# Loading and rounding v by GpSimd, a chunk of four units at a time

## The chip, the core and the metric

The kernel runs on one core of a Trainium2 chip. The core has five engines with a queue of instructions each: TensorE (PE in the profile; its weight loads are PEld), VectorE (DVE), ScalarE (ACT), GpSimd (POOL) and SyncE (SP). Each queue is worked off in order, and engines wait for one another by semaphores. Sixteen DMA engines, common to all queues, move data between device memory and the on-chip memory. The metric is device microseconds of one execution, lower is better; the profile is one execution seen by the hardware profiler.

## What is computed

Two layers follow each other. The first is a linear attention with a decaying state, over batch 4, 8 heads, 768 steps and a head dimension of 48:

```python
for t in range(S):
    cur = np.einsum('bhd,bhe->bhde', u[None] * kt, vt)
    y[:, :, t] = np.einsum('bhd,bhde->bhe', rt, state + cur)
    state = wt[:, :, :, None] * state + np.einsum('bhd,bhe->bhde', kt, vt)
```

The second takes y as 3072 tokens of 384 features and computes h = y w_in (384 to 1024), solu = h softmax(h), a layer norm of solu with gains g_ln, and the product with w_out (1024 to 384). All inputs and the output are float32 in device memory.

## The kernel before

The 768 steps are cut into six chunks of C = 128, and a chunk of one batch is a *unit*: 24 units, unit i being chunk i // 4 of batch i % 4. In a unit the 128 steps lie on the partitions, and the 8 heads times 48 features, 384 columns, along the free axis. Four units in a row are thus one chunk of all batches. The state st of a batch goes from one of its units to the next.

For each unit the kernel loads w, k, r and v (192 KB each, in pieces of 48 float32, 192 bytes). The rows in order of work, with the stage's name in the program: lw takes the logarithm of w (ACT); cum sums it with two matmuls, ex exponentiates (ACT) and kp multiplies into k and r (DVE); krk and krr transpose on PE and kr copies the result (DVE or ACT). M makes the scores, m copies them with the causal mask, on DVE in one step or on ACT with the mask sel behind it on POOL. p, q and qh on POOL and dg on DVE make the bonus term r·u·k of each head and step, and dv (POOL) multiplies it into v. Y is the attention output on PE: it reads the masked scores and v, and for a unit marked `i` also dv by a matmul; otherwise dv is added in the copy y on DVE. S is the new state on PE, with v as its moving operand, and et and st end it. X and xT transpose y, H is the first product of the second layer, e its exponential (ACT), he the product (DVE), hq the square, ea a half sum of e (POOL), Oa and Ob the second product with the sums of the norm, sq, qm, lv and o the norm, and out the store (SP).

v goes through two stages of its own. LV is a load by SP into one of seven float32 buffers v_in, and vb a rounding copy into one of ten bf16 buffers vb. A suffix in the order says which engine makes the copy: 12 on POOL (`vb2.p`), six on DVE (`vb1.d`), six on ACT (`vb0.a`). Readers of vb are S, Y and dv (lines 360, 406 and 434).

Nothing is scheduled by a compiler. One string, ORDER (lines 21 to 67), lists every stage of every unit, and the loop at its end (lines 550 to 553) emits them one by one. The class InOrder (lines 72 to 90) makes each instruction follow the last of its own engine, so each engine's queue has the order of the string. That is why most rows of the profile bear line 86, the line in InOrder that makes the call: a row is told by the tiles that it writes and reads, not by its line. A stage that comes too early in the string makes its engine wait with everything behind it. All loads and stores stand in SP's queue, in the order of the string, and a load waits there until its buffer is free.

Around the start of the string, SP's loads are LW2, LU0, LW1, LW3, LR2, LK2, LV2, LR1, LK1, LW0, LV1, LW4, LG0, LR0, LK0, LR3, LK3, LR4, LV0, LK4, then the weights (LI, LO), then LV3, LW6, LV4 and so on. Unit 2 is the first to be computed, then 1 and 0.

Of the kernel before, what the change touches and what calls it, by code (L numbers as in the profile page):

```python
# [8 lines left out]
F32 = mybir.dt.float32  # L9
BF16 = mybir.dt.bfloat16  # L10
# [10 lines left out]
ORDER = """  # L21
LW2 LU0 ik0 lw2 hot5.4 cum2.0 LW1 lw1 us0.7 ih0 LW3 lw3 cum3.2 LR2 uc0 ex2 LK2 p2 LV2 vb2.p kp2 hot4.4 krk2.6 krr2
LR1 LK1 cum1.4 LW0 ex1 kp1 kr2.d hot1.0 S2.7 lw0 et2 LV1 vb1.d LW4 st2 p1 q1 hot2.0 krk1.1 krr1 q2 qh2 dg2 LG0
kr1.a M2.4 ex3 hot1.0 M1.6 m1.d dv2 LR0 LK0 p0 q0 cum0.0 ex0 lw4 cum4.6 ex4 kp0 krk0.1 krr0 LR3 gs0.0 gc0 dg1
m2.d Y2.i0 kr0.d LK3 p3 LR4 LV0 vb0.a dg0 dv1 kp3 Y1.i5 hot3.1 krk3.4 krr3 LK4 kp4 M0.2 m0.d krk4.1 y1.a X1.5
krr4 y2.a X2.0 dv0 xT2.d hot1.6 Y0.n7 y0.d kr3.a M3.2 hot1.0 X0.6 S1.4 p4 q3 kr4.a xT1.a xT0.a LI2 LI1 wi1.a
M4.0 m4.a et1 LI0 S0.5 et0 wi0.d m3.d LO1 wi2.p H1.6 e1 gw5.a H2.0 e2 H0.2 LO0 gw2.a q4 qh4 dg4 qh3 dg3 gw4.p
gw7.p LV3 vb3.p dv3 sel4 LW6 e0 gw6.d st1 LV4 vb4.p he1 lw6 dv4 gw1.d LW5 gw0.d gw3.d mn0.4 mc0 ce5.p ce6.p
Y3.i7 ce4.p he2 st0 he0 cum6.0 y3.a ce7.p hot1.5 X3.6 lw5 xT3.a ce3.d LK6 LR6 p6 Y4.n5 LR5 LK5 ce2.d hq0.a ex6
LW7 cum5.2 H3.6 p5 y4.d ex5 ce1.d ce0.d Oa0.5 kp6 krk6.1 krr6 S4.0 hq1.d Oa1.4 kp5 krk5.3 krr5 X4.2 Ob1 e3 he3  # L30
LV5 q6 q5 kr5.d hq2.a et4 st4 M5.6 kr6.a M6.0 xT4.d lw7 cum7.2 hq3.a sq1 m6.a m5.d dg5 vb5.d qm1 dv5 Ob0 ex7 sq0
qm0 S3.7 qh6 LR7 LK7 p7 kp7 et3 lv1 st3 lv0 H4.0 Y5.n6 y5.d LR9 LK8 o1.d e4 krk7.3 krr7 Oa2.2 he4 X5.7 q7 kr7.d
LW9 lw9 o0.a LK9 p9 LW8 lw8 S5.6 et5 cum9.4 ex9 Ob2 sq2 LR8 p8 st5 dg6 kp9 qm2 LV6 xT5.a LV9 vb6.p dv6 sel6
cum8.0 ex8 kp8 hq4.a LV7 LV11 out1 LW10 dg7 vb7.p dv7 Oa3.3 vb9.a lv2 H5.6 e5 M7.4 m7.d he5 q8 krk9.1 LK10 krr9
kr9.a S9.0 et9 Ob3 sq3 st9 q9 qm3 o2.a out0 ea5.p Y6.i5 y6.a LV8 LR10 Y7.n4 y7.d LW11 LW12 krk8.1 M9.6 lw10 lv3
X6.2 xT6.a m9.d o3.a krr8 LV10 out3 out2 kr8.d qh9 dg9 dg8 hq5.d cum10.4 ex10 kp10 S6.0 vb11.d et6 X7.2 xT7.a
st6 p10 vb8.d dv8 dv9 H6.6 e6 he6 H7.2 lw11 e7 he7 M8.4 m8.a Oa5.1 Y9.n0 Ob5 sq5 y9.d cum11.6 ex11 krk10.5 krr10
qm5 kr10.d S7.4 et7 st7 Oa4.3 hq6.d lv5 lw12 o5.a X9.2 sel8 Y8.i0 vb10.p y8.a LK11 LR11 kp11 xT9.d q10 dg10 p11
M10.4 m10.a sel10 S10.1 et10 st10 dv10 S8.0 et8 S11.7 et11 X8.6 xT8.a LK12 LW13 cum12.4 q11 ex12 lw13 st11 st8
Ob4 sq4 qm4 LW14 LR12 kp12 p12 lw14 lv4 o4.a out5 LK13 LV12 LR13 Y10.n2 dg11 y10.d H8.6 e8 krk12.1 krk11.0 krr11  # L40
krr12 kr12.d he8 kr11.a q12 qh12 cum13.4 H9.2 vb12.p S12.1 ex13 p13 q13 ea7.p dg12 kp13 dv11 LW16 LR14 LK14 e9
he9 et12 st12 M12.6 m12.a Oa6.0 X10.5 xT10.a krk13.4 krr13 kr13.a M11.6 m11.d ea8.p dv12 sel12 p14 cum14.2 ex14
q14 out4 Ob6 sq6 hq8.d M13.4 m13.d LV13 hq7.a LW15 lw15 lw16 kp14 vb13.d H10.6 dg13 qm6 LW18 lw18 Y11.n1 y11.d
Oa8.5 LK16 LR15 LR16 LK15 e10 he10 hq9.a krk14.4 Y12.i3 krr14 lv6 qh14 kr14.d p15 ea10.p dv13 LR18 LV14 vb14.p
q15 qh15 LK18 p18 Ob8 sq8 qm8 y12.a S13.2 et13 st13 o6.a lv8 X11.1 xT11.d cum16.6 ex16 X12.3 hq10.d LW19 kp16
Oa9.4 cum15.0 xT12.a Ob9 ex15 kp15 sq9 o8.a dg14 dv14 qm9 M14.2 m14.a sel14 krk16.7 Oa7.6 krr16 kr16.d lv9 o9.d
cum18.0 ex18 kp18 Ob7 LV15 S14.5 et14 st14 krk15.3 krr15 kr15.d LK19 Y13.i2 lw19 cum19.0 krk18.7 p16 q16 vb15.a
S15.4 y13.a sq7 qm7 dg15 X13.5 xT13.d ex19 LR19 kp19 lv7 o7.a q18 krr18 kr18.d H11.2 et15 st15 krk19.5 krr19
kr19.d LW17 lw17 cum17.0 e11 he11 ex17 ea11.p out8 LK17 LR17 p17 kp17 H12.6 e12 he12 hq11.a p19 H13.4 e13 Oa10.3
Y14.n2 M16.0 m16.a dg16 q19 dv15 y14.d ea12.p ea13.p M15.6 m15.d he13 Ob10 sq10 X14.2 out9 Oa11.1 LW20 qm10 lw20  # L50
cum20.6 hq12.d krk17.0 krr17 out6 out7 LV16 vb16.a dv16 xT14.a S16.2 LR20 ex20 LK20 dg18 et16 st16 lv10 o10.a
H14.4 e14 kp20 Ob11 sq11 kr17.d LK23 qm11 lv11 o11.a Oa12.2 krk20.3 krr20 kr20.a he14 sel16 Y16.n7 y16.d Y15.n6
y15.d M19.4 m19.a M18.0 m18.d Ob12 X15.7 xT15.a q17 hq13.d LV19 LW21 LV17 X16.3 xT16.a ea14.p vb19.a M17.4 m17.d
sq12 LK22 out10 qm12 dg17 qh19 vb17.p sel19 p20 hq14.a LW22 LV20 q20 qh20 dv17 M20.0 LV21 m20.d out11 LK21 H15.6
e15 he15 lw22 ea15.p H16.4 LV18 vb18.p dv18 LR21 p21 lw21 Oa14.3 Y17.n1 LR22 LV23 q21 dg19 dv19 Ob14 LR23 p23
p22 e16 he16 lv12 Oa13.0 LW23 o12.a out12 sq14 qm14 hq15.d vb20.a lv14 dg20 dv20 y17.d cum21.6 ex21 Ob13 cum22.4
sq13 ex22 LV22 vb22.p ea16.p o14.d out14 Y18.n2 y18.d Oa15.1 X18.3 qm13 kp22 lv13 xT18.d X17.2 xT17.a kp21 Ob15
sq15 qm15 S18.5 et18 st18 Y19.n4 y19.d lv15 o15.a out15 o13.a krk22.2 S17.3 et17 lw23 H18.6 e18 ea18.p hq16.d
vb21.d st17 Y20.n5 y20.d X19.4 xT19.d krr22 kr22.a H17.0 he18 hq18.d cum23.4 ex23 kp23 Oa16.3 e17 ea17.p he17
krk21.2 krr21 kr21.a H19.6 e19 krk23.5 X20.4 krr23 q22 qh21 vb23.p out13 xT20.a kr23.a he19 Oa18.2 Ob16 sq16  # L60
M21.0 q23 ea19.p qh23 dg22 dv22 m21.a sel21 qm16 lv16 M22.6 hq19.a M23.4 Ob18 sq18 dg21 H20.0 o16.a out16 m22.d
m23.d Oa19.7 Y22.n6 qm18 lv18 hq17.d Ob19 S19.5 dg23 dv23 e20 Oa17.4 y22.d X22.3 he20 et19 st19 xT22.d dv21
Y21.n6 Ob17 y21.d sq19 o18.a sq17 qm17 lv17 Y23.n1 out18 qm19 lv19 X21.0 xT21.d H22.2 o17.a e22 out17 ea20.p
y23.d H21.0 X23.5 xT23.a e21 hq20.d o19.d out19 Oa20.6 he22 hq22.d H23.4 e23 he21 hq21.d Ob20 sq20 qm20 lv20
o20.a out20 ea22.p Oa22.7 ea21.p Oa21.3 he23 hq23.d Ob22 sq22 qm22 lv22 Ob21 sq21 qm21 lv21 o21.d o22.a out22
out21 ea23.p Oa23.2 Ob23 sq23 qm23 lv23 o23.a out23
"""

NIO, NLW, NKP, NWK = 7, 10, 6, 4
# [24 lines left out]
def kernel(  # L94
# [26 lines left out]

    nc.scalar.preload_act_table_set("natural_log_exp_and_others")
# [27 lines left out]
    v_t = ring("v_in", NIO, [C, H, 64], F32)  # L150
# [4 lines left out]
    g_rows = consts.tile([KF, 128], F32)  # L155

# [41 lines left out]
    vb_t = ring("vb", NLW, [C, H, D], BF16)  # L198
# [15 lines left out]
    qm_t = ring("qm", NWK, [C, 1], F32)  # L214
    lv_t = ring("lv", NWK, [C, 1], F32)
# [30 lines left out]
    def load_w(i, x):  # L246
        sp.dma_start(out=w_t[i % NIO][:, :, :D], in_=rows_of(w, i))

    def load_k(i, x):
        sp.dma_start(out=kr_t[i % NIO][:, 0, :, :D], in_=rows_of(k, i))  # L250

    def load_r(i, x):
        sp.dma_start(out=kr_t[i % NIO][:, 1, :, :D], in_=rows_of(r, i))

    def load_v(i, x):
        sp.dma_start(out=v_t[i % NIO][:, :, :D], in_=rows_of(v, i))

    def load_u(i, x):
        sp.dma_start(out=u_row, in_=u.rearrange("(o h) d -> o (h d)", o=1))

    def load_g(i, x):
        sp.dma_start(out=g_rows, in_=moe_g_ln.rearrange("(ko ki) -> ko ki", ki=128))

    def load_w_in(j, x):
        sp.dma_start(out=win_f[:, j, :], in_=moe_w_in[j * 128:(j + 1) * 128, :])

    def load_w_out(j, x):
        part = slice(j * KF // 2, (j + 1) * KF // 2)
        sp.dma_start(out=wout_f[:, part, :],
                     in_=moe_w_out.rearrange("(ko ki) d -> ki ko d", ki=128)[:, part, :])  # L270
# [79 lines left out]
    def v_cast(i, x):  # L350
        copy = {"a": act.copy, "d": dve.tensor_copy, "p": pool.tensor_copy}[x]
        copy(out=vb_t[i % NLW], in_=v_t[i % NIO][:, :, :D])

# [4 lines left out]
    def bonus_v(i, x):  # L358
        dg = dg_t[i % NWK]
        pool.tensor_mul(out=dv_t[i % NKP], in0=vb_t[i % NLW], in1=dg.unsqueeze(2).to_broadcast([C, H, D]))  # L360
# [16 lines left out]
    def transposed_copy(i, x):  # L377
        copy = {"a": act.copy, "d": dve.tensor_copy}[x]
        copy(out=kr_s[i % NKP], in_=live[i]["kr_ps"])

# [22 lines left out]
    def attend(i, x):  # L403
        L = live[i]
        c, b = units[i]
        m, kr, vb = m_t[i % NWK], kr_s[i % NKP], vb_t[i % NLW]
        y_ps = L["y_ps"] = bank([C, DM], F32, x[-1], "y_ps")
        first = True
        if x[0] == "i":
# [67 lines left out]
    def hidden_exp(i, x):  # L477
        act.activation(out=e_t[i % NWK], in_=live[i]["h_ps"], func=EXP)
# [105 lines left out]
```

## Time and profile before

| what | value |
|---|---|
| median of 2 runs | 155.07 us (154.83 to 155.32) |
| span of the profiled execution | 152.4 us |
| what lies around the span, by the median of the runs | 155.07 - 152.4 = 2.7 us |
| granted TensorE clock, mean over the span | 0.975 |
| DMA queue of SP | 104,802 packets, 26.75 MB, 77.4% of 16 engines' span |
| of these, packets of v | 24 loads of 128 x 8 pieces = 24,576 |
| copies vb on POOL, 12 | 6.3 us, mean 522 ns |
| copies vb on DVE, 6 | 3.8 us, mean 635 ns |
| copies vb on ACT, 6 | 3.1 us, mean 510 ns |
| v loads, issue to landing | 3.6 us median, 3.1 to 6.7 |

The profile gives no time of the profiled execution but its span, from the first instruction to the last; the runs' times are longer by what lies around it. In the profile "idle before" is the time that an engine stood still ahead of an instruction, with what ended that wait. The chain that ended last is followed back from the last instruction, at each step to what released it. DMA shares can go above 1 in a stretch, because records of packets overlap.

### The profile page before, as it was taken

Reading aid. Unit: us, or ns where it says so; the run is one execution under the profiler, and the core shown is the slowest. Engines: PE = TensorE matmul, PEld = TensorE weight load, DVE = VectorE, ACT = ScalarE, POOL = GpSimd, SP = SyncE. Lnnn points to the kernel's source line nnn. Section 1 sums busy time; section 2 is a strip of 40 time slices with the busy share of each in tenths; the row PEclk is TensorE's granted clock in tenths of the full one; section 3 lists DMA queues with packets and bytes.
Section 4 is the critical chain, followed back from the end, with each engine's and each line's share of the span. In section 5 each row is a group of like instructions: output and inputs, shape, how many; then the busy total and the mean of one; then the engine's idle time right before and its main releaser. Section 6 shows DMA issues by size and latency. Waiting matters only on the chain.

```text
span 152.4 us, 5172 instructions
## 1 busy us (share of the span) xinstructions
PE 136.4 (90%) x2093; PEld 105.5 (69%) x2093; DVE 131.8 (87%) x227; ACT 120.0 (79%) x247; POOL 119.0 (78%) x149
## 2 busy tenths in 40 slices
PE   6777598968999999999998999999799999999970
PEld 1242365936778889779776689887686988889740
DVE  5029968899999999998999999999999999988940
ACT  4526648869888999799998889998988789938661
POOL 7268986799909994899999997799889979973600
PEclk9959969999999999999999999999999999999998
DMA  3999999989979999989897989995998110112023
GB/s 76 218 216 211 217 334 377 254 175 223 216 151 216 220 204 229 206 177 224 194 203 144 228 195 275 199 199 136 241 205 210 63 45 4 44 63 103 4 79 127
DMA packets 104825, 27.06 MB, mean 178 GB/s; under 512 B 100314, under 2 KB 104419, under 8 KB 104803
## 3 DMA queue, kind: packets, MB, share of 16 engines
q1 hardware_dynamic: 104802, 26.75, 77.4%
q8 instruction: 16, 0.26, 0.7%
q14 instruction: 7, 0.05, 0.1%
HBM read 22.03 MB, written 4.72 MB: 176 GB/s over the span
## 4 chain that ended last, share of the span: by engine, by line
PE 53%; DVE 23%; SPq 8%; ACT 6%; issue 3%; DMA 2%; POOL 1%; DVEq 0%; POOLq 0%
PE ps L86 53%; SPq L86 7%; DVE he L86 6%; DVE m L86 4%; DVE kp L86 4%; DVE w L86 3%; DMA kr_in<-in_k_dram 2%; DVE kr L86 1%; DVE hq L86 1%; DVE y L86 1%; DVE st L86 1%; ACT ps L86 1%; ACT o L86 1%; DVE dg L86 1%; ACT win_sb L86 1%
## 5 line engine op out<-in xcount | busy, mean ns | idle before, releaser
L86 PE MATMUL ps<-w,he 128*128 128x385 bf16 x192 | 44.5, 325 | 1.0 <-DVE w L86 0.7
L86 PE MATMUL ps<-xT,win_sb 128*128 128x128 bf16 x576 | 35.5, 219 | 1.1 <-DVE qm L86 0.8
L86 PEld LDWEIGHTS <-win_sb 128*128 128x128 bf16 x576 | 32.8, 98 | 2.2 <-DVE m L86 0.9
L86 PE MATMUL ps<-one_col,hq 128*128 128x1 bf16 x192 | 31.5, 164 | 0.0
L86 DVE TENSOR_TENSOR he<-ps,e 128x1024 bf16<-128x1024 f32 x24 | 29.1, 1214 | 1.6 <-ACT e L86 1.6
L86 DVE TENSOR_TENSOR kp<-ps,kr_in 128x768 bf16<-128x768 f32 x24 | 22.8, 951 | 7.7 <-DMA kr_in<-in_k_dram 4.9
L86 POOL TENSOR_TENSOR p<-kr_in 128x384 bf16<-128x384 f32 x24 | 24.7, 1038 | 4.5 <-DMA kr_in<-in_k_dram 4.2
L86 POOL TENSOR_TENSOR dv<-vb,dg 128x384 bf16<-128x384 bf16 x24 | 21.7, 907 | 7.5 <-DVE qm L86 3.6
L86 ACT ACTIVATE e<-ps 128x1024 bf16<-128x1024 f32 x24 | 24.5, 1021 | 3.1 <-PE ps L86 2.0
L86 POOL TENSOR_TENSOR ea<-e 128x512 bf16<-128x512 bf16 x17 | 20.0, 1181 | 6.4 <-ACT e L86 5.7
L86 POOL TENSOR_TENSOR q<-p,u_bc 128x384 bf16<-128x384 bf16 x24 | 22.2, 931 | 2.4 <-DVE dg L86 1.7
L86 ACT ACTIVATE ps<-ps 128x768 f32<-128x768 f32 x24 | 19.1, 799 | 5.1 <-PE ps L86 4.3
L86 PEld LDWEIGHTS <-kp 128*128 128x128 bf16 x272 | 17.5, 100 | 6.0 <-DVE kp L86 3.2
L86 PEld LDWEIGHTS <-he 128*128 128x128 bf16 x192 | 18.4, 96 | 4.0
L86 PEld LDWEIGHTS <-hq 128*128 128x128 bf16 x192 | 15.4, 96 | 8.3
L86 DVE TENSOR_TENSOR m<-ps,keep 128x1024 bf16<-128x1024 f32 x15 | 18.2, 1216 | 1.2 <-PE ps L86 1.0
L86 PE MATMUL ps<-ident,kp 128*128 128x128 bf16 x192 | 16.5, 227 | 1.6 <-POOL p L86 1.1
L86 DVE TENSOR_TENSOR hq<-he 128x1024 bf16<-128x1024 bf16 x15 | 13.4, 890 | 0.1
L86 ACT COPY kr<-ps 128x1024 bf16<-128x1024 bf16 x11 | 11.1, 1012 | 2.4 <-PE ps L86 2.4
L86 ACT ACTIVATE lw<-w_in 128x384 bf16<-128x384 f32 x23 | 11.7, 523 | 1.3 <-DMA w_in<-in_w_dram 1.3
L86 PEld LDWEIGHTS <-kr 64*128 64x128 bf16 (+1 forms) x272 | 10.2, 95 | 3.1 <-ACT kr L86 0.7
L86 PE MATMUL ps<-inv_col,ea 128*128 128x1 bf16 x68 | 11.2, 165 | 0.0
(90 smaller groups left out, 293.7 us busy)
## 6 DMA issues: line engine op xcount, KB each, us to landing
w_in<-in_w_dram SPq DMA_DIRECT2D x24, 192.0 KB, 3.7
kr_in<-in_r_dram SPq DMA_DIRECT2D x24, 192.0 KB, 3.7
kr_in<-in_k_dram SPq DMA_DIRECT2D x24, 192.0 KB, 3.7
v_in<-in_v_dram SPq DMA_DIRECT2D x24, 192.0 KB, 3.6
out_dram<-o SPq DMA_DIRECT2D x24, 192.0 KB, 2.6
win_f<-in_moe_w_in_dram SPq DMA_DIRECT2D x3, 512.0 KB, 6.4
wout_f<-in_moe_w_out_dram SPq DMA_DIRECT2D x2, 768.0 KB, 9.0
u_row<-in_u_dram SPq DMA_DIRECT2D x1, 1.5 KB
```

The lines of the kernel that those rows point to most:

```text
L86: made = make(*args, **kwargs)
```

## The change

v is no longer loaded by SP and rounded by three engines. For each of the six chunks, one transfer in POOL's queue takes the v of all four units, 128 steps x 32 rows (batch and head) x 48 features, 768 KB of float32, and writes bf16 straight into one of four buffers of 128 x 32 x 48. A unit's vb is a slice of such a buffer.

```diff
-NIO, NLW, NKP, NWK = 7, 10, 6, 4
+NIO, NLW, NKP, NWK, NHT, NVG = 7, 10, 6, 4, 4, 4
...
-    v_t = ring("v_in", NIO, [C, H, 64], F32)
...
-    vb_t = ring("vb", NLW, [C, H, D], BF16)
+    vb_g = ring("vb", NVG, [C, B * H, D], BF16)
+    vb_t = [vb_g[j // B % NVG][:, j % B * H:(j % B + 1) * H, :] for j in range(NU)]
...
-    def load_v(i, x):
-        sp.dma_start(out=v_t[i % NIO][:, :, :D], in_=rows_of(v, i))
+    def load_v(c, x):
+        pool.dma_start(out=vb_g[c % NVG], in_=v.rearrange("b h t d -> t (b h) d")[c * C:(c + 1) * C])
...
-    def v_cast(i, x):
-        copy = {"a": act.copy, "d": dve.tensor_copy, "p": pool.tensor_copy}[x]
-        copy(out=vb_t[i % NLW], in_=v_t[i % NIO][:, :, :D])
...
-        pool.tensor_mul(out=dv_t[i % NKP], in0=vb_t[i % NLW], in1=dg.unsqueeze(2).to_broadcast([C, H, D]))
+        pool.tensor_mul(out=dv_t[i % NKP], in0=vb_t[i], in1=dg.unsqueeze(2).to_broadcast([C, H, D]))
...
```

In the order string the 24 words LV and the 24 words vb are gone, and six words LV0 to LV5, one for each chunk, are put in:

```diff
+LW2 LU0 ik0 LV0 lw2 hot5.4 ...
+... H0.2 LO0 gw2.a q4 LV1 qh4 dg4 qh3 dg3 gw4.p gw7.p dv3 ...
+... q7 kr7.d LW9 lw9 o0.a LK9 LV2 p9 LW8 lw8 S5.6 ...
+... LK11 LR11 kp11 xT9.d q10 dg10 LV3 p11 M10.4 ...
+... LW17 lw17 cum17.0 e11 he11 ex17 LV4 ea11.p out8 ...
+... H15.6 e15 he15 lw22 ea15.p H16.4 LV5 dv18 LR21 ...
```

All other words keep their order. The second instruction of the stage lv has become a stage rs, and each rs follows its lv directly, so that the instructions stay the same. The changed file also has stages that its order does not use (transposes by DMA, a second layout of H) and a choice of the queue for other loads, which is left at SP everywhere.

## The prediction

> **What bounds the kernel now.** I read the page's busy times first, then sums by stretch, then the chain that ended last, then the queues of POOL, PE and SP around each place where the change puts or takes a word. The page's first part:
>
> ```profile
> PE 136.4 (90%) x2093; PEld 105.5 (69%) x2093; DVE 131.8 (87%) x227; ACT 120.0 (79%) x247; POOL 119.0 (78%) x149
> ```
>
> No engine has much room. Sums by stretch (busy us of each engine, granted clock, share of the DMA engines, GB/s) tell where it is:
>
> ```profile
> 3.80:11.00 7.20, 5.22 (x29) 2.60 (x29) 0.96 (x1) 2.77 (x6) 2.76 (x8) 0.81 1.08 216
> 11.00:17.20 6.20, 3.97 (x42) 1.96 (x41) 5.64 (x9) 4.14 (x8) 5.43 (x7) 0.95 1.06 210
> ...
> 43.00:60.00 17.00, 16.94 (x301) 14.18 (x296) 16.73 (x30) 15.73 (x38) 13.05 (x16) 1.00 0.94 203
> 60.00:75.00 15.00, 15.00 (x263) 12.23 (x261) 14.29 (x26) 13.77 (x30) 13.04 (x16) 1.00 0.97 204
> 75.00:95.00 20.00, 19.23 (x308) 15.43 (x305) 19.48 (x33) 18.27 (x41) 18.90 (x21) 1.00 0.96 205
> 95.00:110.00 15.00, 14.54 (x261) 12.07 (x258) 14.95 (x20) 13.80 (x27) 14.19 (x15) 1.00 0.93 195
> ```
>
> To 17 us the DMA engines are full (1.08, 1.06) and the others wait. From 43 us PE is full or nearly so, DVE beside it. The chain (start, us, what) agrees:
>
> ```profile
> 13.35 3.79 DMA kr_in<-in_k_dram
> 17.14 0.03 POOLq L86
> 17.17 0.18 POOL q L86
> 17.34 0.07 issue
> 17.41 0.99 POOL p L86
> 18.41 0.80 POOL dv L86
> ...
> 43.27 31.86 PE ps L86 x551
> ...
> 80.44 0.92 DVE vb L86
> ...
> 90.21 0.40 ACT vb L86
> ...
> 110.34 37.23 PE ps L86 x601
> ```
>
> The start hangs on LK3's landing at 17.14, which lets POOL do p3 and then dv1, for which PE waits. Later, of 24 rounding copies, two stand on the chain.
>
> **What is removed.** 12 x 0.522 = 6.3 us of POOL, 6 x 0.635 = 3.8 us of DVE, 6 x 0.51 = 3.1 us of ACT, and 24 issues of SP. From 43 to 110 us PE idles 17 - 16.94 + 0 + 0.77 + 0.46 = 1.3 us, so a faster DVE or ACT cannot bring more than that there; on the chain stand 0.92 + 0.40 = 1.3 us. PE's work is late next, at once. I take **-0.8** (0 to -1.3).
>
> **The start.** LV0 stands behind POOL's constants and masks, near 3.2 us, and is in flight with SP's first loads. The packets stay as many: 24 x 1024 before, 6 x 4096 after, 192 bytes each. But ahead of LK3 SP had two loads of v; now four go. From 9.37 to 17.14 (landings of LR1 and LK3) eight loads of 192 KB land, 0.97 us each with the small LG0 among them; I take 0.9. That it is the DMA engines and not SP that pace them: an issue into an idle queue takes 0.43 us (first w, or v at 52.4), a back-to-back one 0.7 to 1.1. Two loads more are **+1.8** at p3, dv1 and Y1 behind them; dv1 ends 0.05 us before PE takes it, so nothing hides it. Bounds: 0 if SP's packets go first; 2.7 if LK1, behind one v load before and four now, sets the pace.
>
> **What one transfer holds POOL for.** The trace has no transfer in POOL's queue. The nearest row is SP doing the same 4096 pieces of v, four loads in a row, at 44.68:
>
> ```profile
> 44.68 3.51 SPq L86 DMA_DIRECT2D v_in<-in_v_dram  x4
> ...
> 52.40 0.43 SPq L86 DMA_DIRECT2D v_in<-in_v_dram  x1
> ```
>
> That is 3.5 us. Below: POOL's p takes 1038 ns for 384 columns, 2.7 ns a step; if one step writes a piece for each of 16 DMA engines, 256 steps are 0.7 us. Above: one step for one piece, 4096 x 2.7 = 11.1 us. Nothing excludes either; a gain is excluded, since the queue must do something. I take 3.5 us, the row with the same count and bytes.
>
> At each LV everything behind it on POOL is late by 3.5 us less the casts gone, less POOL's idle time, less the slack that the timelines show between POOL's end and its reader's start. LV0: POOL idles 2.98 us before p2, which is late itself; 0. LV1 at 24.4: qh4 would end 2.1 us before dg4; 1.4 us late on DVE, which idles 0.7 before the next he; 0.7 lost. LV2: under the wait below. LV3 at 65.3: dv8 had waited 2.66 us for a cast on DVE, which goes, and a POOL cast too; 0. LV4 at 93.7: two casts (1.0) and idle 0.77 + 0.81 lie between it and sel16, whose slack is 0.42; 3.5 - 1.0 - 1.6 - 0.4 = 0.5. LV5 at 114.3: two casts (1.0) and idle 0.94 just before it; 1.6 late, dv18's slack is 0.5; 1.1. Sum **+2.3** (0 at 0.7 us a transfer; the upper end is a rival).
>
> **The new wait.** A unit's v is there only when its chunk's whole transfer is. I compared each LV's place on POOL with its first reader: LV1 24.4, dv4 33.3; LV3 65.3, S12 73.3; LV4 93.7, S16 101.3; LV5 114.3, dv20 120.7 with the DMA engines at 0.44. But LV2 stands between these two rows of POOL, and S9 in PE's queue is its reader:
>
> ```profile
> 47.79 0.91 POOL L86 TENSOR_TENSOR q<-p,u_bc 128x384 bf16<-128x384 bf16 x1
> 48.67 1.96 POOL L86 TENSOR_TENSOR p<-kr_in 128x384 bf16<-128x384 f32 x2
> ```
>
> ```profile
> 53.61 0.33 PE L86 MATMUL ps<-vb,kp 128*128 128x96 bf16 x4
> ```
>
> A lead of 4.9 us. The four v loads at 44.68 issued their last at 47.1, and the slowest of the four landed 4.9 us after issue: 52.0, or 7.3 us for the bytes of one LV. By that LV2 lands at 56.0 and S9 is **+2.4** late; behind S9 in PE's queue stand Ob3, Y6 and all else, and PE has no idle time to give it back (15.00 of 15.00). The other leads, 6.4 to 8.9, cover 7.3, LV5's for the emptier DMA. Bounds: nothing if it lands within 4.9; with half of 210 GB/s, 786,432 / 105,000 = 7.5 us and the 2.3 us that a lone load's 3.2 us has beyond its own data, 9.8, so 4.9 late.
>
> The Trainium skill, "DMA: Bandwidth & Descriptors" (section Anatomy of one DMA), puts a GpSimd transfer at about 2.0 us plus bytes at 436 GB/s, an estimate of 3.8 us for 786,432 bytes, and holds that many descriptors can be emitted before their cost shows. By that S9 would not wait and the term would be 0; the trace's 203 to 216 GB/s with pieces of 192 bytes speak for about half its rate.
>
> **Sum.** -0.8 + 1.8 + 2.3 + 2.4 = +5.7 on 155.1 (span 152.4 and 2.7 around it, the runs' median): **160.8 us**. Its own range by the bounds: 156 to 167. A change within 2% (152.0 to 158.2) is about what cannot be told from none.
>
> **Rivals.**
> *Hidden after all (0.20).* A transfer holds POOL about 1 us and LV2 lands within 4.9 us; the start costs 0 to 1.8 and 0.8 is saved: 154.3 to 156, taken as 155. For it: POOL idles in some places, and the leads are long but one. Against: the full DMA engines.
> *Faster (0.08).* If SP's issuing paced the start, two v issues of 0.99 and 1.11 us leave the way to LK3, and the chain's 1.3 us of casts go: 155.1 - 3.4 = 151.7. Against: shares of 1.08 and 1.06.
> *POOL becomes the bound (0.26).* Between 25 and 135 us POOL idles some 13 us, and 6.3 us of casts go; five transfers use that up from about 4 us each. At 11.1 us they add 5 x 11.1 - 19 = 36, and LV0, 11.1 less 3 hidden, 8: about 199. At 6 us, 30 - 19 = 11, 3 at the start, and 3 to 5 of waits for data: 173. The place is dv, sel and qh late for PE and DVE at each LV. The skill's "SBUF — State Buffer" (section SBUF: two separate sides) names a way to it: GpSimd cannot write descriptors while VectorE holds their shared port. The trace has hints of sharing: DVE's casts of one shape took 345 to 1000 ns.
> *Slow packets (0.06).* If rounding doubles a packet's time (0.774 x 152.4 x 16 / 104,802 = 18 ns on average), v counts twice on the DMA engines; a share of 0.95, with v 24,576 of 104,802 packets, becomes 0.95 x 1.23 = 1.17, over some 75 us: +13, 168.
> That the change doesn't do what it says is excluded: the new POOL queue has six transfers of 128 x 32 x 48 and no cast.
>
> **How the numbers follow.** Forecast 0.40, rivals as above. Below 154 lie the faster case and a little of the hidden one (0.11), above 185 the worst third of the POOL case (0.09): range 154 to 185. Faster by over 2%: 0.07, of the faster case. Within 2%: 0.25, the hidden case and 0.05 of the forecast. Slower: 0.68.
>
> **What would show it.** POOL's queue with six issues of some 3.5 us, and POOL's idle time behind them; LK3 landing near 19 us and dv1 near 21; PE idle for 2 us before S9, put down to a DMA into vb; DVE about 4 us and ACT 3 us less busy. Wrong if an issue is far from 3.5 us, if the landing of LV2 is far from 7.3 us after POOL reaches it, or if POOL comes to a later LV much earlier or later than before.

## The result and the profile after

The changed kernel takes 172.05 us (median of two runs, 170.82 and 173.27) against 155.07 before: a ratio of 1.110 [1.091, 1.129], or 17 us more. The forecast was 160.8, in a range of 154 to 185. The profiled execution is the run of 170.82 us, with a span of 168.8. (Medians and ranges take in all runs; ratios leave out runs over 1.5% above the fastest of their kernel, and where only one run is left, 166.91 us for "Chunk 0 as before" and 156.40 us for "Chunk 0 as before and earlier words", there is no ratio.)

The page of the changed kernel: busy time of each engine, the chain's shares, the two DMA queues (packets, MB, share of 16 engines' span), and the row of the new transfers with the median time from issue to landing.

```profile
PE 141.0 (84%) x2091; PEld 107.9 (64%) x2093; DVE 130.3 (77%) x221; ACT 118.3 (70%) x241; POOL 123.1 (73%) x143
...
q1 hardware_dynamic: 79842, 22.03, 61.1%
q0 software_dynamic: 24672, 2.36, 26.2%
...
PE 34%; DMA 27%; DVE 18%; POOL 7%; ACT 6%; issue 5%; DVEq 0%; POOLq 0%; ACTq 0%
...
vb<-in_v_dram POOLq DMA_DIRECT2D x6, 384.0 KB, 11.0
```

No engine has become the bound: every share has fallen, PE's from 90% to 84%, POOL's from 78% to 73%. What is new is 27% of DMA on the chain, and 11.0 us from issue to landing. (PE's 4.6 us more of busy time go with a mean granted clock of 0.96, 0.975 before.) The instructions that write or read vb, with their shortest, median and longest duration in ns:

```profile
L84 POOL DMA_DIRECT2D vb<-in_v_dram x6: 1737/1746/1885, 3.2 to 130.8; - x6
...
DMA to landing us min/median/max: 7.0/11.0/11.9
```

So POOL is held 1.75 us for each transfer, half of the 3.5 us that I took, and the data arrive 7.0 to 11.9 us after the issue, not 7.3. The sums by stretch, with the columns as before:

```profile
3.80:11.00 7.20, 5.73 (x19) 2.24 (x19) 0.96 (x1) 2.52 (x5) 3.59 (x9) 1.00 1.45 159
11.00:17.20 6.20, 3.36 (x24) 2.00 (x21) 2.11 (x3) 1.38 (x3) 3.15 (x4) 1.00 1.33 170
...
43.00:60.00 17.00, 14.43 (x241) 11.63 (x240) 15.45 (x25) 14.25 (x29) 14.51 (x16) 1.00 0.89 128
60.00:75.00 15.00, 11.17 (x175) 9.03 (x175) 8.41 (x14) 7.89 (x18) 5.79 (x7) 0.77 0.76 126
75.00:95.00 20.00, 17.47 (x282) 13.94 (x280) 15.66 (x24) 15.86 (x34) 18.11 (x20) 0.91 1.19 170
95.00:110.00 15.00, 14.88 (x234) 12.03 (x234) 14.49 (x27) 13.28 (x32) 12.81 (x14) 1.00 0.79 176
```

PE was busy 15.00 of 15.00 us in the fourth row before; now it is 11.17, and part of that at a granted clock of 0.77. (GB/s of the two kernels can't be compared directly: a rounding transfer is counted with its bf16 bytes, half of what it reads. The same times also hold later words in the kernel before.) The chain names what PE waits for (start, us, what):

```profile
3.19 11.92 DMA vb<-in_v_dram
15.11 0.04 issue
15.15 2.20 PE ps L84 x14
...
52.04 11.74 DMA vb<-in_v_dram
63.79 0.04 issue
63.83 6.76 PE ps L84 x99
...
75.87 11.49 DMA vb<-in_v_dram
...
107.35 10.47 DMA vb<-in_v_dram
...
134.06 30.33 PE ps L84 x499
```

Four of the six transfers stand on it: LV0, LV2, LV3 and LV4. In PE's timeline the one that had been forecast, S9, reads (in brackets the idle time ahead and what ended it):

```profile
63.83 0.48 PE L84 MATMUL ps<-vb,kp 128*128 128x96 bf16 x4 [6.40 <-DMA vb<-in_v_dram]
```

Where the 17 us come from is seen by comparing when the same words start in the two traces (us from the start of the span):

| word on PE | before | after | late by | added since the row above | wait for vb there |
|---|---|---|---|---|---|
| S2 | 10.9 | 15.2 | 4.3 | 4.3 | 2.8 |
| S4 | 39.8 | 44.0 | 4.2 | -0.1 | |
| S9 | 53.6 | 63.8 | 10.2 | 6.0 | 6.4 |
| S12 | 73.3 | 87.4 | 14.1 | 3.9 | 2.3 |
| S16 | 101.3 | 117.9 | 16.6 | 2.5 | 1.6 |
| Y20 | 121.3 | 138.2 | 16.9 | 0.3 | |
| end of the span | 152.4 | 168.8 | 16.4 | -0.5 | |

All of it is added at, or just behind, the first readers of LV0, LV2, LV3 and LV4. The waits alone are 13.2 us of the 16.4. A part of the rest is the clock; PE's busy time, granted clock and DMA share in the stretches around S9:

```profile
57.00:64.00 7.00, 0.60 (x12) 0.38 (x10) 1.99 (x2) 1.23 (x2) 5.75 (x7) 0.71 1.57 169
64.00:66.00 2.00, 2.00 (x18) 1.14 (x17) 0.56 (x1) 0.35 (x3) 0.00 (x0) 0.50 0.12 25
66.00:68.00 2.00, 2.00 (x43) 1.79 (x42) 0.85 (x3) 1.63 (x5) 0.00 (x0) 0.81 0.03 8
```

After the stall the next 2 us run at a clock of 0.50 and the two behind them at 0.81: 2 x 0.50 + 2 x 0.19 = 1.4 us lost. After the wait of 2.3 us at S12 the same happens (0.50 for 2 us, 0.68 for 2 us: 1.6 us); after the 1.6 us at S16 the clock stays at 1.00. So S12's 3.9 us are about 1.4 of clock and 2.3 of waiting, and S16's 2.5 are 1.6 of waiting and 0.9 that are left of the clock's loss behind S12.

### The profile page after: what moved, and what is told of

Same layout as the page of the kernel before. It is cut to its first block, busy times and chain, and to the rows that moved or that the text cites. A ratio compares the mean times of both kernels' runs of the same rounds, so it can differ in the third digit from the quotient of the medians.

```text
span 168.8 us, 5133 instructions
## 1 busy us (share of the span) xinstructions
PE 141.0 (84%) x2091; PEld 107.9 (64%) x2093; DVE 130.3 (77%) x221; ACT 118.3 (70%) x241; POOL 123.1 (73%) x143
## 3 DMA queue, kind: packets, MB, share of 16 engines
q0 software_dynamic: 24672, 2.36, 26.2%
## 4 chain that ended last, share of the span: by engine, by line
PE 34%; DMA 27%; DVE 18%; POOL 7%; ACT 6%; issue 5%; DVEq 0%; POOLq 0%; ACTq 0%
PE ps L84 34%; DMA vb<-in_v_dram 27%; DVE m L84 4%; DVE kp L84 3%; DVE he L84 3%; DVE w L84 2%; POOL q L84 2%; ACT e L84 2%; POOL dv L84 1%; DVE hq L84 1%; DVE win_sb L84 1%; ACT kr L84 1%; POOL vb L84 1%; DVE st L84 1%; DVE kr L84 1%
## 5 line engine op out<-in xcount | busy, mean ns | idle before, releaser
L84 PE MATMUL ps<-w,he 128*128 128x385 bf16 x192 | 45.8, 331 | 0.9 <-DVE w L84 0.7
L84 POOL TENSOR_TENSOR p<-kr_in 128x384 bf16<-128x384 f32 x24 | 25.4, 1064 | 9.6 <-DMA kr_in<-in_k_dram 7.1
L84 POOL TENSOR_TENSOR dv<-vb,dg 128x384 bf16<-128x384 bf16 x24 | 20.2, 845 | 15.2 <-DVE dg L84 9.7
L84 PEld LDWEIGHTS <-kp 128*128 128x128 bf16 x272 | 18.4, 103 | 19.8 <-issue 14.7
L84 PE MATMUL ps<-ident,kp 128*128 128x128 bf16 x192 | 17.1, 232 | 1.3 <-POOL p L84 1.1
L84 PE MATMUL ps<-vb,kp 128*128 128x96 bf16 x80 | 7.1, 214 | 13.2 <-DMA vb<-in_v_dram 13.2
L84 DVE TENSOR_TENSOR st<-ps,et 128x384 bf16<-128x384 f32 x20 | 10.8, 549 | 8.4 <-ACT et L84 8.4
```

The source lines that it names most:

```text
L84: made = make(*args, **kwargs)
```

## Why a landing takes 11 us

The packet records of the trace tell the six landings apart. The rate counts v with the float32 bytes that are read:

| transfer | issue to first packet | first to last packet | last packet to landing | SP's packets meanwhile | read by both, GB/s |
|---|---|---|---|---|---|
| LV0 | 3.1 us | 8.5 us | 0.3 us | 4616 | 196 |
| LV1 | 2.5 | 6.8 | 0.3 | 3750 | 220 |
| LV2 | 2.7 | 8.7 | 0.3 | 4279 | 203 |
| LV3 | 3.0 | 8.1 | 0.4 | 4105 | 196 |
| LV4 | 3.0 | 7.1 | 0.4 | 3774 | 210 |
| LV5 | 2.4 | 4.3 | 0.3 | 144 | 230 |

A transfer has 4096 packets, one for each piece of 48 numbers. While it is in flight, about as many of SP's packets go through (3750 to 4616), and together they reach 196 to 220 GB/s, much as the 195 to 216 of before. Only LV5, with SP quiet, is done in 4.3 us; twice that is 8.6, near the 8.1 to 8.7 of LV0, LV2 and LV3. So the trace fits engines that take turns between the two queues, one packet each: v gets half the rate for 7 to 9 us, and so do SP's loads, whatever is needed first. That they take turns is inferred from these counts; the run without rounding below shows that the rule isn't as simple for larger packets. Before, all were in one queue, in the order of need. (The Trainium skill, "DMA: Bandwidth & Descriptors", section SWDGE vs HWDGE vs iDMA, says that transfers issued by GpSimd and by SP feed different queues inside each DMA engine, which takes turns between them; the counts in this table agree.)

One reading has to be put aside. By the profile's page a packet of GpSimd's lasts 0.262 x 168.8 x 16 / 24,672 = 28.7 ns, and SP's packets before lasted 18 ns on average. But LV5 moves 256 packets per engine in 4.3 us, one each 16.7 ns: the records overlap, and their length is no rate. Some expectations below still count with it.

## The experiments

Three theories, as they stood before the experiments. **Lead**: what costs is the landing time against the distance from the transfer's word to its first reader, at LV0 for the start and at LV2 to LV4 for the rest. **Packets**: rounding during the transfer makes many slow packets, which is what the landing time is. **POOL**: GpSimd, held for the transfers, is what is late. Each time below is a median, with the ratio to the kernel before on the same chip.

### Earlier words

LV2 to LV5 stand earlier (in the traces POOL reaches them at 42.8, 59.2, 88.0 and 108.7 us, not at 52.0, 75.9, 107.4 and 130.8); LV0 and LV1 stay.

```diff
-... LK9 LV2 p9 ...        +... LK6 LR6 LV2 p6 ...
-... dg10 LV3 p11 ...      +... o2.a out0 LV3 ea5.p ...
-... ex17 LV4 ea11.p ...   +... kr14.d p15 LV4 ea10.p ...
-... H16.4 LV5 dv18 ...    +... X15.7 xT15.a LV5 q17 ...
```

> LV2 to LV5 stand earlier in POOL's queue (before p6, ea5, ea10, q17), 15 us or more ahead of their first reader; LV0 and LV1 stay. Theory lead (the loss behind the start is one transfer's 11 to 12 us to landing against leads of 5 to 8 us): PE's waits for vb at S9, S12 and S16 (6.4, 2.3 and 1.6 us in the changed kernel) go, some 12 us come back, 159 to 161 us. Rival contention (packets of 29 ns crowd SP's loads wherever the transfer stands): the waits move to k, r and w, and the time stays above 166 us.

Measured: 157.37 us, 1.018 [1.013, 1.024], less than the 159 to 161 expected. Of the 17 us, 14 to 15 are gone. The waits of PE for vb in its trace, with the sum, how many, and the longest:

```profile
PE ps L83 <- DMA vb<-in_v_dram: 3.2, 1, 3.2
```

One is left, S2's at the start. The landings have not changed (9.1 to 12.1 us), only the leads: S9 now starts 14 us after LV2's issue. So the lead theory holds for nearly the whole cost, and a POOL that is held as often and as long costs little beside it; what it does cost is seen further below.

### LV2 alone

```diff
-... LK9 LV2 p9 ...        +... LK6 LR6 LV2 p6 ...
```

> The changed kernel with LV2 alone moved, from ahead of p9 to ahead of p6 in POOL's queue, some 11 us earlier. Theory lead: S9's wait of 6.4 us goes, and with it the 1.4 us of TensorE clock lost behind the wait (0.50 and 0.81 granted in the 4 us after it): 164 to 166 us. Rival contention: LV2's packets then hold up the loads of k, r and w for units 5 to 9, PE waits for those, and 169 us or more stay.

Measured: 166.22 us, 1.076 [1.067, 1.086]; 5 to 6 us back, about what S9 had added. S9 starts at 56.7 without a wait, and the next one grows, from 2.31 us to

```profile
80.04 0.48 PE L83 MATMUL ps<-vb,kp 128*128 128x96 bf16 x4 [3.38 <-DMA vb<-in_v_dram]
```

which is PE's timeline of this run. Each wait is a cost of its own place. Without the wait at S9, POOL issues LV3 8.4 us earlier (67.4 us, 75.9 after the change) and PE is ready for S12 8.4 us earlier (76.7, 85.1), so the lead is 9.2 us in both; the wait is longer because LV3's landing takes 12.6 us here and took 11.5 there.

### Chunk 0 as before

The first four units are loaded by SP and rounded one by one as before, with Lv for such a load; LV1 to LV5 as in the change.

```diff
-LW2 LU0 ik0 LV0 lw2 ...
+LW2 LU0 ik0 lw2 ... LK2 p2 Lv2 vb2.p kp2 ... et2 Lv1 vb1.d LW4 ... LR4 Lv0 vb0.a dg0 ... gw7.p Lv3 vb3.p dv3 ...
```

> Units 0 to 3 get their v as in the kernel before (four SP loads, four casts at their old words); LV1 to LV5 stay as in the changed kernel. If the 4.3 us that S2 is later are LV0's, they come back in full: S2 near 10.9 us and 167 to 168 us in all. Rival: the later waits for LV1 and LV2 take the gain back because SP's other loads are late as well, 170 to 172 us.

Measured: 171.28 us, from 166.91 to 172.30 in four runs. The profile (of a run of 170.34) shows what it was for: S2 is back at 10.5 us (10.9 before the change, 15.2 after it). So the start's 4.3 us are LV0's: by the trace after, S2 could have run at 12.3 us (1.4 late, with SP's loads slowed beside LV0) and then waited 2.8 us for LV0 itself. But PE still waits at S9,

```profile
61.10 0.48 PE L83 MATMUL ps<-vb,kp 128*128 128x96 bf16 x4 [6.22 <-DMA vb<-in_v_dram]
```

nearly as long as after the change. How much of the start's gain is left at the end isn't settled by the one run of 166.91 us.

### No rounding in the transfer

The same six transfers at the same words, to float32; the 24 casts are back at their old words.

```diff
+    NVF = 2
+    vf_g = ring("v_in", NVF, [C, B * H, D], F32)
...
-        pool.dma_start(out=vb_g[c % NVG], in_=v.rearrange("b h t d -> t (b h) d")[c * C:(c + 1) * C])
+        pool.dma_start(out=vf_g[c % NVF], in_=v.rearrange("b h t d -> t (b h) d")[c * C:(c + 1) * C])
...
+    def v_cast(i, x):
+        copy = {"a": act.copy, "d": dve.tensor_copy, "p": pool.tensor_copy}[x]
+        copy(out=vb_t[i], in_=vf_g[i // B % NVF][:, i % B * H:(i % B + 1) * H, :])
```

> The same six transfers in POOL's queue at the same words, but float32 to float32 without rounding, and the 24 casts at their old words. Theory rounding (29 ns a packet is the price of rounding on the way): packets of 192 bytes near 15 to 18 ns as in SP's queue, landing in 7 to 9 us, 163 to 167 us in spite of 6.3 us of casts on POOL. Rival queue (GpSimd's queue itself is slow): 28 to 29 ns, 11 us to landing, 172 us or more.

Measured: 174.85 us, 1.132 [1.124, 1.141]: slower than the change. That is the time of the rival (172 or more), but not by its slow packets. Its page and its waits:

```profile
q0 software_dynamic: 1248, 4.72, 11.2%
...
v_in<-in_v_dram POOLq DMA_DIRECT2D x6, 768.0 KB, 8.2
```

```profile
ACT vb L84 <- DMA v_in<-in_v_dram: 14.2, 3, 7.6
...
POOL dv L84 <- DVE vb L84: 5.7, 1, 5.7
```

Without rounding, the queue joins its pieces: 192 packets of up to 22 pieces (4.2 KB) in place of 4096, and in flight it takes 65 to 100% of the bytes and is done in 3.9 to 4.9 us instead of 4.3 to 8.7. So the share grows with the size of the packets, though less than turns of one packet each would make it: beside the 192 packets of one transfer 995 to 2207 of SP's pass, nearly all of 192 bytes (none beside LV5), 5 to 11 for each. What sets the share stays open. The landing is still 6.9 to 8.9 us, since nearly 3 us pass before the first packet, and the casts stand ahead of S9 in their engines' queues and wait there with all that is behind them: the shorter landing met a shorter lead. That the cost needs the rounding is therefore wrong; that rounding makes the landing longer beside other loads is shown.

The same with the words of the first experiment, and rows of 64 (48 of them filled) in the buffer:

> As e1 (LV2 to LV5 early, LV0 and LV1 where they are), but the six transfers of GpSimd write float32 in rows of 64, so that a packet stays 192 bytes and nothing is rounded on the way, and the 24 casts are back at their old words. If the price of the crowding is the rounded packet of 96 bytes (28.5 ns against 15.5): packets of 15 to 18 ns, landing 2 to 3 us sooner than in e1, and 154.5 to 156 us but for LV0 and LV1, whose casts now wait in ACT's and POOL's queues (1 to 3 us). If it is the queue of GpSimd as such: packets near 28 ns, landing as in e1, 158 us or more.

Measured: 159.98 us, 1.031 [1.019, 1.043]. I had expected packets of 192 bytes; the queue joined 22 pieces into one (1248 packets in all, as in the last run). The landings are 6.3 to 8.1 us, nothing waits for a landing of v, and the kernel is no faster than the first experiment; the casts are back and POOL is busy 129.1 us against 121.9. On its chain (start, us, what) stands the holding of POOL by LV3, ahead of ea5:

```profile
57.32 1.74 POOL q L84 x2
59.06 0.06 POOL v_in L84
59.12 1.65 issue
60.76 1.17 POOL ea L84
```

### Twenty-four transfers of one unit

Each unit by a rounding transfer of its own, placed one by one ahead of its readers.

```diff
-    vb_g = ring("vb", NVG, [C, B * H, D], BF16)
-    vb_t = [vb_g[j // B % NVG][:, j % B * H:(j % B + 1) * H, :] for j in range(NU)]
+    vb_r = ring("vb", 12, [C, H, D], BF16)
+    vb_t = [vb_r[j % 12] for j in range(NU)]
...
-        pool.dma_start(out=vb_g[c % NVG], in_=v.rearrange("b h t d -> t (b h) d")[c * C:(c + 1) * C])
+        pool.dma_start(out=vb_t[c], in_=rows_of(v, c))
```

> 24 transfers of one unit each in POOL's queue, rounding, each some 8 us or more ahead of its reader. If the 1.75 us of POOL are by the piece, a transfer holds POOL 0.45 us and lands in about 5 us: 155 to 160 us. If they are mostly a fixed cost of the transfer, 1 us or more each, 24 us or more of POOL against 6.3 us of casts gone: 165 us or more.

Measured: 169.33 us, 1.097 [1.092, 1.102]. The instructions on vb, with ns as above, and the landings:

```profile
L84 POOL DMA_DIRECT2D vb<-in_v_dram x24: 881/937/1090, 3.2 to 132.3; - x24
...
DMA to landing us min/median/max: 3.1/4.6/12.3
```

0.94 us for 1024 pieces and 1.75 for 4096 give 0.27 us more per 1024 pieces and, on a straight line through these two, 0.67 us for a transfer of none, an estimate. Twenty-four of them hold POOL for 22.8 us, the casts on it were 6.3, no instruction waits for a DMA into vb, and POOL has 30% of the chain (7% after the change). So the rival in which POOL becomes the bound is real at 24 transfers and absent at six.

### Chunk 0 as before and earlier words

The edits of both: Lv and vb for the first four units, and LV2 to LV5 at their earlier words.

> Chunk 0 as in the kernel before (four SP loads, four casts), LV1 where it is, LV2 to LV5 15 us or more ahead. If start and lead are all of the loss, what is left is LV1's landing (dv4 waited 2.0 us) and the gain of the casts (0.8 us): 153 to 155.5 us, within 1% of the kernel before. If transfers of GpSimd cost by crowding the other loads as well, 157 us or more.

Measured: 160.68 us, from 156.40 to 163.97 in six runs. Not the 153 to 155.5 expected, and, without a ratio, not to be told from earlier words alone (157.37); no more follows from it.

### Chunks 0 and 1 as before, and earlier words

The same, with the units 4 to 7 loaded and rounded one by one as well, so that LV1 is gone too.

```diff
-... gw2.a q4 LV1 qh4 ...
+... gw7.p Lv3 vb3.p dv3 ... st1 Lv4 vb4.p he1 ... he3 Lv5 q6 ... dg5 vb5.d ... qm2 Lv6 xT5.a vb6.p ... hq4.a Lv7 out1 ... vb7.p dv7 ...
```

> Chunks 0 and 1 as in the kernel before, LV2 to LV5 early. Lead and start theory: no transfer of GpSimd falls into the stretch to 43 us where the DMA engines are full, 153 to 154.5 us, equal to or below the kernel before by up to 1%. If the gain of the 16 casts is taken up by the four times 1.75 us on POOL: 154.5 to 156.

Measured: 158.16 us, 1.025 [1.017, 1.033]. A miss: the start is regained (S2 at 10.8) and no PE instruction waits for v, but the end is as late as in the first experiment. The chain of this run has the new cost:

```profile
41.59 1.40 SPq L83
43.02 8.49 DMA w_in<-in_w_dram
...
112.81 2.13 SPq L83
114.99 6.80 DMA w_in<-in_w_dram
```

Two of SP's loads of w, 3.7 us at the median of the kernel before, take 8.5 and 6.8 us. Both are in flight with a transfer of v: LV2 from 38.9 to 51.3 and LV5 from 108.4 to 120.3. In the last run of this section, where SP alone loads, the same two take 3.4 and 3.9 us. So a transfer by GpSimd lengthens SP's loads beside it.

That is not all that is left: POOL is also held for 1.75 us where it has no time. Between 40 and 130 us three waits of PE are over 0.5 us: 0.67 us behind the first of these loads, and two that lead back to POOL. The longer of these two, at H15, is 2.08 us, where PE waited 0.78 in the kernel before: hq13 on DVE, ahead of it, takes 2.88 us in place of 1.58, beside work of POOL that stands behind LV5. (In the five traces with LV5 at its earlier word hq13 takes 2.87 to 3.32 us, in that of the last run 1.58; that POOL's work is the reason isn't tested by itself.) The other is M8, for kp10 on DVE:

```profile
64.64 0.40 PE L83 MATMUL ps<-kr 64*128 64x128 bf16 x8 [1.93 <-DVE kp L83]
```

Ahead of kp10, dg9 on DVE stood idle 1.83 us for qh9 on POOL, and qh9 stands behind these two:

```profile
58.78 1.74 POOL L83 DMA_DIRECT2D vb<-in_v_dram  x1
60.55 1.17 POOL L83 TENSOR_TENSOR ea<-e 128x512 bf16<-128x512 bf16 x1
```

The first experiment and the float32 one with its words have both waits too (M8 1.42 and 1.52 us, H15 2.08 and 2.52); the kernel before does not wait at M8. These are single traces, of runs 1 to 2% longer than their medians. Three runs try the causes.

**LV3 elsewhere.** The same, with LV3 ahead of dv8 and no longer ahead of ea5.

```diff
-... out0 LV3 ea5.p ...        +... st6 p10 LV3 dv8 ...
```

> e8 with LV3 moved from ahead of ea5, where the chain of e1 shows POOL's held time ahead of ea5, to ahead of dv8, where POOL had waited 2.7 us in the kernel before; S12 is still some 12 us away. If POOL held at a bad place is part of e8's loss: 1 to 2 us less than e8, 156 to 157. If crowding is all of it: 157.5 to 159, as e8.

Measured: 158.78 us, 1.022 [1.015, 1.028], beside 1.025 [1.017, 1.033]: no gain that can be told, though the intervals leave room for one of 1%. In its trace M8 no longer waits, so that wait was POOL's holding by LV3; but the wait behind the load of w is 2.33 us there and H15's is 2.08 again.

**No transfer by GpSimd.** SP loads chunks 2 to 5, four loads in a row ahead of LW9, LK11, LW17 and LK21, and POOL rounds each chunk in one copy of 1536 columns per partition at the change's words (CV). Such a copy takes 1.46 us in the traces of both forms, not the 1.9 expected. Chunks 0 and 1 as before. In its first form the copies of chunks 2 and 4 stood ahead of their loads in the order, and so took the former contents of the buffer:

> No transfer of GpSimd at all: SP loads v of each unit as before (chunks 2 to 5 four in a row, earlier), chunks 0 and 1 are cast as before, and chunks 2 to 5 by one POOL copy each of 128 x 32 x 48, about 1.9 us, at the words of LV2 to LV5. It takes the 16 casts away and holds POOL as long as the transfers do, without their packets. If crowding on the DMA engines is what e8 still loses: 153.5 to 155, like the kernel before. If it is POOL held for 1.75 us at a time: 157 to 159, like e8.

It took 171.58 us, which says nothing on the question, since the loads waited behind the copies. With the loads ahead:

```diff
+... q7 kr7.d LV8 LV9 LV10 LV11 LW9 ... LK9 CV2 p9 ... y8.a LV12 LV13 LV14 LV15 LK11 ... dg10 CV3 p11 ...
...
+        sp.dma_start(out=vf_g[c // B % NVF][:, c % B * H:(c % B + 1) * H, :D], in_=rows_of(v, c))
...
+    def chunk_cast(c, x):
+        pool.tensor_copy(out=vb_g[c % NVG], in_=vf_g[c % NVF][:, :, :D])
```

> No transfer of GpSimd at all: SP loads v of each unit as before (of chunks 2 to 5 four in a row, earlier, ahead of LW9, LK11, LW17 and LK21), chunks 0 and 1 are cast as before, and chunks 2 to 5 by one POOL copy each of 128 x 32 x 48, about 1.9 us, at the words of LV2 to LV5. It takes 16 casts away and holds POOL as long as the transfers do, without their packets. If crowding on the DMA engines is what e8 still loses: 153.5 to 155, like the kernel before. If it is POOL held for 1.75 us at a time: 157 to 159, like e8.

Measured: 159.05 us, 1.017 [1.007, 1.028] (156.57 to 159.28, and one run of 429.56, in which PE was busy for 420 us; that was the profiled one, so its waits tell nothing here). A residue is there with no transfer by GpSimd at all. Two possible causes remain: the chunk copy on POOL, or the four loads in a row.

**Only the loads moved.** The kernel before, with its 24 casts at their words; the loads of chunks 2 to 5 stand as in the last one, in buffers of a chunk.

```diff
+... kr7.d LV8 LV9 LV10 LV11 LW9 ... y8.a LV12 LV13 LV14 LV15 LK11 ... kr19.d LV16 LV17 LV18 LV19 LW17 ... out11 LV20 LV21 LV22 LV23 LK21 ...
```

> The kernel before, with all its 24 casts at their old words and no transfer on GpSimd; only the loads of v of chunks 2 to 5 are moved: four SP loads in a row, at the places where the former test without GpSimd transfers had them (ahead of LW9, LK11, LW17 and LK21). It differs from that test, which stood at 1.017 [1.007, 1.028], in one thing: GpSimd isn't held for a whole chunk's rounding. Theory that fetching a chunk of v at once takes the DMA engines from nearer loads of w, k and r: it stays near that test, 1.012 to 1.02, 157 to 158 us, with waits of DVE's kp or POOL's p for loads near these places. Rival, that GpSimd's holding of 1.7 to 1.9 us at a time is what is left: it is as fast as before, 0.995 to 1.005, 154.2 to 155.8 us.

Measured: 156.62 us, 1.0136 [1.0109, 1.0164]. So without any change on POOL, fetching v a chunk at a time, and earlier, costs 1.4%, nearly what the run with POOL's chunk copies cost (1.017). SP's timeline and DVE's show one such place:

```profile
58.34 2.92 SPq L84 DMA_DIRECT2D v_in<-in_v_dram  x4
61.31 0.74 SPq L84 DMA_DIRECT2D kr_in<-in_k_dram  x1
62.10 0.97 SPq L84 DMA_DIRECT2D kr_in<-in_r_dram  x1
```

```profile
66.52 0.96 DVE L84 TENSOR_TENSOR kp<-ps,kr_in 128x768 bf16<-128x768 f32 x1 [0.82 <-DMA kr_in<-in_r_dram]
```

The load of r stands behind four of v, and kp on DVE, which waited for nothing there before, waits 0.82 us for it; PE, busy 15.00 us from 60 to 75 before, is busy 14.22. This is a load that stands behind others in SP's one queue. In the runs with GpSimd's transfers no load stands behind v there, so their residue (1.8 to 2.5%) is something else: by the traces above, SP's loads that are longer beside a transfer, and POOL held by it. How the residue divides between the two isn't settled by the times.

No version tried is faster than the kernel before.

## Why the prediction was right, and where its sizes were off

The direction was right, and so were a late start and a new wait at S9. The size was not: +5.7 was forecast and +17 measured. The sum's own range, 156 to 167, is missed (and the bounds of its terms add up to 153.8 to 165.0, not to that). The stated range of 154 to 185 holds 172 only because of a rival, POOL becoming the bound, that isn't what happened; that is luck. By its terms:

- **What is removed, -0.8.** Not seen by itself. DVE's busy time fell by 1.5 us and ACT's by 1.7, not by about 4 and 3 as forecast; what else grew there isn't settled.
- **The start, +1.8: measured +4.3.** The mechanism was v ahead of LK3 on full DMA engines. LK3 landed at 19.98 us (2.8 later than the 17.14 of before; near 19 was forecast) and dv1 ran at 21.9 (near 21). But I looked for the delay at Y1 and missed the nearer reader, and it sets the loss: S2, the first to read vb, waits for all of LV0 (11.9 us), where before it needed LV2 of one unit. So the wait for a whole chunk, forecast at S9, had no term at S2. And SP's queue was held up beside the transfer; two loads of w, 0.75 and 0.70 us to issue before, now take

```profile
7.11 4.35 SPq L84 DMA_DIRECT2D w_in<-in_w_dram  x2
11.50 2.49 SPq L84 DMA_DIRECT2D g_rows<-in_moe_g_ln_dram  x1
```

- **What one transfer holds POOL for, 3.5 us, +2.3: measured 1.75 us and at most 0.3 us of delay.** POOL's busy time rose by 4.1 us, about what six transfers (10.6) less the casts (6.3) make. SP's time for four loads was the wrong neighbour; 1.75 lies nearer to the lower bound of 0.7, and by the prediction's own working it gives 0 at every LV. One hold does stand on the chain, LV5's ahead of dv18, the place that was forecast to cost 1.1 us:

```profile
130.85 1.67 POOL vb L84
132.55 0.85 POOL dv L84
```

PE, 16.6 us late at S16 before it, is 16.9 us late at Y20 behind it.
- **The new wait at S9, +2.4: measured +6.0.** The place and the queue behind it were right. The step that failed is the landing: 7.3 us, taken from four of SP's loads in a row, in the one queue where later loads stand behind them. Measured were 11.7, with about as many packets of SP's going through meanwhile. The upper bound, half of the DMA rate and 2.3 us besides (9.8 us), had the mechanism, and was still short: 2.7 us before the first packet, 8.7 in flight and 0.3 behind it. The lead, 4.9 us by the two rows of before, was 5.4: 63.83 - 6.40 - 52.04. The Trainium skill's formula on the page "DMA: Bandwidth & Descriptors" (section Anatomy of one DMA), by which this term would have been 0, does not hold here: 3.8 us by the formula, 7.0 measured with SP nearly quiet.
- **The other leads, 0: measured +3.9 at S12 and +2.5 at S16.** "The other leads, 6.4 to 8.9, cover 7.3" followed from the same wrong landing. PE was ready 9.2 us after LV3's issue and 8.9 after LV4's, and the data took 11.5 and 10.5. LV1 took 9.6, and dv4 on POOL waited 2.0 us for it, without making PE later. LV5, with SP quiet, took 7.0 and nothing waits for it, as forecast.
- **A term that was left out: the clock.** A stall of PE costs more than its length, 1.4 us behind S9 and 1.6 behind S12.

Of the rivals, *slow packets* gave 168 and a chance of 0.06; its mechanism isn't it either, since both queues together read 196 to 220 GB/s, as before. *POOL becomes the bound* fell with 1.75 us a transfer; the hold was 1.73 to 2.09 us in all traces of a whole chunk's transfer. *Hidden after all* had POOL's holding nearly right and the landing wrong. *Faster* fell with the start: the first readers came later, not earlier.

## What to carry to other kernels

A load moved to another queue no longer takes its turn by need. While both queues had small packets here, each got about half the rate, so count such a landing at half the rate, plus the time to its first packet, and hold that against the distance to its first reader at every place, not only at the shortest. The loads that stay in the first queue get longer as well. One transfer for four units makes the first of them wait for the last, and brings the data of the later three ahead of loads that are needed sooner; that cost here 1.4% even within one queue. A wait added to an engine without idle time is paid in full, and more when the clock drops behind it. An engine that issues transfers is held by each, and what stands behind it in its queue can keep the busiest engine waiting, as M8 shows.

## What the runs showed of the hardware

- GpSimd's transfers of a chunk: mostly 2.4 to 3.4 us from issue to the first packet (4.3 and 4.5 us for LV1 in the two runs with only chunk 0 as before); POOL held for 0.94 us at 1024 pieces and 1.75 at 4096, both with rounding, and for 1.73 to 1.93 us at 4096 without it.
- A rounding transfer sends each piece of 48 numbers as a packet of its own (24,576 for v); the same transfer without rounding joins up to 22 pieces into a packet of 4.2 KB, and then takes 64 to 100% of the bytes while in flight in place of about half.
- The granted TensorE clock was 0.50 over the 2 us behind a stall of 2.3 us and 0.68 over the next 2, and stayed at 1.00 behind one of 1.6 us. No fixed length divides the two: it fell at stalls of 1.98 and 2.10 us in the trace of "Chunk 0 as before" and not at 2.14 us in "LV2 alone" or 2.29 us in "Twenty-four transfers of one unit". Between 40 and 150 us each low stretch in these traces is 3.41 or 6.83 us long. The Trainium skill, "TensorE: Matmul & The Clock Gate" (section Part 1: The HAM clock gate), puts the drop behind an idle window of about 3.4 us; here 2.0 to 2.3 us were enough in some places.
